# Attention and two expert layers on one core: the first batch's P·v product in plain float32

## The chip, the core and the metric

The kernel runs on one NeuronCore of a Trainium2 chip. TensorE (PE, with its weight loads listed as PEld) multiplies, VectorE (DVE) and ScalarE (ACT) work elementwise, GpSimd (POOL) works elementwise and issues indirect DMAs, and SyncE (SP) issues the other DMAs. The metric is the device time of one execution in microseconds (us).

## The reference

The inputs are q, k and v of 4 batches with 8 heads each, 576 positions and 64 features, and the weights of two feed-forward stages. All of it is float32.

```python
scores = scale * np.matmul(q, k.transpose(0, 1, 3, 2))
scores = np.where(mask, scores, -1000000000.0)      # mask: block_i >= block_j, blocks of 64
scores = scores - np.max(scores, axis=-1, keepdims=True)
attn = np.exp(scores)
attn = attn / (np.sum(attn, axis=-1, keepdims=True) + 1e-09)
out = np.matmul(attn, v)
...
x = out.transpose(0, 2, 1, 3).reshape(B * S, H * D)
x = ((x @ w1) * (x @ w2)) @ w3 @ w_out
...
# then a router (noisy top 2 of 8 experts) and, per expert, relu(x @ w1[e]) @ w2[e], weighted
```

## The kernel before

**Split products.** Most products are made from float32r operands. A float32 matrix is split into a high part (a rounded copy, by ACT) and a low part (the difference, by DVE or POOL), and two or three matmuls of the parts are summed in PSUM (`split`, `mm3`). For P·v two parts of P meet one weight tile that holds v's high part in columns 0 to 63 and its low part in columns 64 to 127, so the output has 128 rows; they go to DRAM (`x2`) and a later stage adds the two halves.

**One head of attention.** `load` and `load_v` bring q, k and v. `prep_h` splits q and k (ACT, DVE L571, POOL L574), `prep_v` splits v (ACT L579, POOL L580). `s_unit` makes the scores of 128 rows of q at a time in PSUM (`sb`, L599 to L602); `s_max` takes the row maxima (DVE L613, and L616 to join two halves) and the exponentials (ACT L618). `g_unit` transposes P in 128x128 tiles into a PSUM bank (`tp`, L629) in four groups and copies each into `pt`: the high part by ACT (L633), the low part by DVE (L639), or, for group 3 of the first eight heads, by a second ACT copy (L636) and POOL (L637). `av_a` and `av_b` multiply (L645, L656): per head six matmul shapes of 128, 448, 448, 320, 192 and 128 columns, each twice, once per part of P. Head numbers 0 to 7 are the first batch.

**Beside the heads.** While the first ten heads run, four times per head (`feed`) a 512 KB piece of the first feed-forward stage's weights is loaded into one of two buffers `stg` (L511), turned from 64-bit to 32-bit words by three DVE instructions (`conv64`, L520 to L522, into `stf`), and split by ACT (L453) and POOL (L457) into `pc`. The product w3·w_out is made from these pieces in 64 units of three 512-column matmuls (`w_unit`). After it the feed-forward stage itself (`Moe1`) fills PE's time between the heads' steps, in chunks of 256 tokens; its inputs `xab`, `xr` come from `x2` and from the sums of the heads of a whole batch.

**The order.** The tables `FIRST` and `LATER` say in what order steps of head i and head i+1 are recorded; a list scheduler then orders each engine's instructions by its own estimates and the priorities given. Each engine runs its list strictly in that order, so an instruction that waits holds up what stands behind it. `buf` places an odd head of the first batch in pool `px`, all others in `p1`.

Of the kernel before, what the change touches and what calls it, by code (L numbers as in the profile page):

```python
# [8 lines left out]
F32 = mybir.dt.float32  # L9
F32R = mybir.dt.float32r  # L10
# [4 lines left out]
OP = mybir.AluOpType  # L15
# [4 lines left out]
B, H, S, D = 4, 8, 576, 64  # L20
NT, DM, DF, E = 2304, 512, 1024, 8
BH = B * H
P = 128
# [23 lines left out]
PTW = 1792  # L47
AV0 = 1280
# [27 lines left out]
def r32(ap):  # L76
    return ap.bitcast(F32)
# [365 lines left out]
class Kernel:  # L443
# [82 lines left out]
    def attention(self):  # L526
        tc, nc, a = self.tc, self.nc, self.a
        moe1 = self.moe1
        with tc.tile_pool(name="p1", bufs=1, side="right") as p1, tc.tile_pool(name="stg", bufs=2, side="right") as self.stg, \
# [13 lines left out]
            px = pxs.enter_context(tc.tile_pool(name="px", bufs=1))  # L543

            def buf(h, shape, dt, name):

                return (px if h < H and h % 2 else p1).tile(shape, dt, name=name)

            pbs = []
            for h in range(2):  # L550
                pbs.append([buf(h, [P, PW[t]], F32, f"pb{t}") for t in range(5)])
                for t in range(5):
                    if PW[t] > KW[t]:
                        nc.gpsimd.memset(pbs[h][t][:, KW[t]:], 0.0)

            def load(h):
                c = hd[h] = Ctx()
                c.qk = buf(h, [P, 2, S], F32, "qk")
                nc.sync.dma_start(c.qk, a["qk"][h])

            def load_v(h):
                c = hd[h]
                c.v = buf(h, [P, 5, D], F32, "v")
                nc.sync.dma_start(c.v, a["v"][h])

            def prep_h(h):
# [8 lines left out]

            def prep_v(h):
                c = hd[h]
                c.vv = buf(h, [P, 5, P], F32R, "vv")
                nc.scalar.copy(c.vv[:, :, 0:64], c.v)  # L579
                nc.gpsimd.tensor_tensor(c.vv[:, :, 64:128], c.v, r32(c.vv[:, :, 0:64]), op=OP.subtract)  # L580

# [39 lines left out]
            def g_unit(h, g):  # L621
                c = hd[h]
                pb = pbs[h < H and h % 2]
                if g == 0:
                    c.pt = buf(h, [P, 2, PTW], F32R, "pt")
                base, skip, items = G_UNITS[g]
                bank = psT.tile([P, 512], F32, name="tp")
                for n, (t, kt) in enumerate(items):
                    nc.tensor.transpose(bank[:, n * P:(n + 1) * P], pb[t][:, kt * P:(kt + 1) * P], self.ident)  # L629
                o = len(items) * P - skip  # L630
                src = bank[:, skip:skip + o]
                h_, l_ = c.pt[:, 0, base:base + o], c.pt[:, 1, base:base + o]
                nc.scalar.copy(h_, src)  # L633
                if h < H and g == 3:
                    gf = px.tile([P, 512], F32, name="gf", bufs=2)[:, 0:o]
                    nc.scalar.copy(gf, src)  # L636
                    nc.gpsimd.tensor_tensor(l_, gf, r32(h_), op=OP.subtract)  # L637
                else:
                    nc.vector.tensor_tensor(l_, src, r32(h_), op=OP.subtract)  # L639

            def av_a(h):
                c = hd[h]
                bank = psT.tile([P, 512], F32, name="tp")
                for i in range(2):
                    nc.tensor.matmul(bank[:, 0:P], c.vv[:, 0, :], c.pt[:, i, AV0:AV0 + P], start=(i == 0), stop=(i == 1))  # L645
                c.ev = buf(h, [P, S], F32, "ev")
                nc.vector.tensor_copy(c.ev[:, 0:128], bank[:, 0:128])  # L647

            def av_b(h, kts):
                c = hd[h]  # L650
                if kts[0] == 0:
                    c.av = psV.tile([P, 512], F32, name="av")
                for kt in kts:
                    _, s0, w, o0 = AV_UNITS[kt]
                    for i in range(2):
                        nc.tensor.matmul(c.av[:, o0:o0 + w], c.vv[:, kt, :], c.pt[:, i, s0:s0 + w],  # L656
                                         start=(kt == 0 and i == 0), stop=(kt == 4 and i == 1))
                if kts[-1] == 4:
                    nc.scalar.copy(c.ev[:, 128:576], c.av[:, 0:448])
                    self.x2w[h] = nc.sync.dma_start(self.x2[h], c.ev)  # L660
# [93 lines left out]

            tick = moe1.tick
            load(0)
            raw += [self.load64(*jobs[n][:2]) for n in range(2)]
            feed()
            prep_h(0)
            load(1)  # L760
            load_v(0)
            feed()
            feed()

            def step(i, j, op):

                kind, n = op[0], op[1:]
                if kind == "f":
                    fill(float(n))
                elif kind == "c":  # L770
                    feed()
                elif kind == "t":
                    tick()
                elif kind == "g" and i >= 0:
                    g_unit(i, int(n))
                elif kind == "p" and i >= 0:
                    prep_v(i)
                elif kind == "a" and i >= 0:
                    av_a(i)
                elif kind == "b" and i >= 0:  # L780
                    av_b(i, [0, 1, 2] if n == "0" else [3, 4])
                elif kind == "s" and j < BH:
                    s_unit(j, int(n))
                    s_max(j)
                elif kind == "h" and j + 1 < BH:
                    prep_h(j + 1)
                elif kind == "v" and 0 < j < BH:
                    load_v(j)
                elif kind == "l" and j + 2 < BH:
                    load(j + 2)  # L790
                elif kind == "o":
                    if i == H - 1 or i > H and i % H == 0:
                        sums_out((i - 1) // H if i > H else 0)
                    if i >= H:
                        moe1.ready = i // H
                    if i == 4:
                        moe1.setup_dram(0)
# [225 lines left out]
```

## Time and profile before

| what | value |
|---|---|
| median of 3 runs | 1152.62 us (1151.78 to 1153.02) |
| the profiled execution's own time | 1154.8 us |
| its span, first to last instruction | 1152.9 us |
| PE busy | 1059.8 us (92%), 6588 matmuls |
| DVE busy | 588.2 us (51%) |
| ACT busy | 503.5 us (44%) |
| POOL busy | 384.8 us (33%) |
| mean granted TensorE clock | 0.966 |

Busy shares are averages over the whole span; a stage has its own. PE's busy time counts matmuls that overlap each other in the pipeline, so it overstates how full PE is. The granted clock is a share of 2.4 GHz; the two levels seen are 1.0 and 0.5.

### The profile page before, as it was taken

The numbers are of one execution on the slowest core, as the hardware profiler recorded it, in microseconds if no ns is written. First come the engines' busy times: TensorE is split into PE (matmuls) and PEld (weight loads), VectorE is DVE, ScalarE is ACT, GpSimd is POOL, SyncE is SP. The second block draws the span as 40 slices with busy tenths as digits, with TensorE's granted clock in tenths as the row PEclk, the third lists the DMA queues.
The fourth block names the chain that finished last, engine by engine and source line by source line (L and its number), as shares of the span: only waits on it lengthen the run. The fifth ranks groups of instructions, "written<-read, shape, count | busy, mean of one in ns | idle before, by whom it ended". The sixth has DMA issues, their size and how long they took to land.

```text
span 1152.9 us, 17651 instructions
## 1 busy us (share of the span) xinstructions
PE 1059.8 (92%) x6588; PEld 951.2 (83%) x6588; DVE 588.2 (51%) x1253; ACT 503.5 (44%) x1196; POOL 384.8 (33%) x369
## 2 busy tenths in 40 slices
PE   4698978998999987999899988999999999999996
PEld 3486767897898967998888887998989898989894
DVE  5989997765485735645433642542424242424120
ACT  4765565564465635553223432533333333333220
POOL 4654555424242423422322325413131313120202
PEclk8899979999899988999999999999999999999999
DMA  8654586324622355313522317736263626351303
GB/s 243 199 167 165 158 225 196 96 82 91 191 92 83 95 153 138 88 54 91 92 56 37 129 47 230 211 105 150 78 154 89 158 81 150 83 131 28 45 5 44
DMA packets 75347, 135.82 MB, mean 118 GB/s; under 512 B 15885, under 2 KB 41717, under 8 KB 75253
## 3 DMA queue, kind: packets, MB, share of 16 engines
q1 hardware_dynamic: 65141, 113.44, 34.0%
q0 software_dynamic: 10112, 21.16, 9.8%
q8 instruction: 54, 0.88, 0.3%
q14 instruction: 40, 0.33, 0.1%
HBM read 103.92 MB, written 30.66 MB: 117 GB/s over the span
## 4 chain that ended last, share of the span: by engine, by line
PE 66%; DVE 12%; DMA 12%; issue 3%; ACT 2%; POOL 1%; SPq 0%; POOLq 0%; DVEq 0%; ACTq 0%
PE ph L462 12%; PE ph L463 12%; PE ph L464 12%; PE m L462 6%; PE m L463 6%; PE m L464 6%; DMA xr<-rs 3%; PE tp L629 2%; PE av L656 2%; DVE stf L521 2%; DMA stg<-in_w_dram 2%; PE sb L602 2%; DVE hi L571 1%; PE m L871 1%; DVE stf L522 1%
## 5 line engine op out<-in xcount | busy, mean ns | idle before, releaser
L462 PE MATMUL m<-xh,pc 128*128 128x256 f32 x576 | 165.9, 292 | 4.0 <-DVE at L204 3.6
L463 PE MATMUL m<-xh,pc 128*128 128x256 f32 x576 | 163.2, 287 | 0.0
L464 PE MATMUL m<-xh,pc 128*128 128x256 f32 x576 | 163.0, 287 | 0.0
L462 PE MATMUL ph<-xt,pc 128*128 128x256 f32 (+1 forms) x512 | 157.1, 309 | 4.9 <-ACT xt L453 4.9
L463 PE MATMUL ph<-xt,pc 128*128 128x256 f32 (+1 forms) x512 | 157.4, 307 | 0.0
L464 PE MATMUL ph<-xt,pc 128*128 128x256 f32 (+1 forms) x512 | 157.1, 307 | 0.0
L898 POOL DMA_INDIRECT out_dram<-yo,ids x40 | 64.1, 1603 | 202.7 <-ACT yo L897 104.2
L884 DVE SCALAR_TENSOR_TENSOR ht<-ph,ht 128x256 fp32r<-128x256 f32 (+1 forms) x128 | 61.8, 490 | 132.7 <-ACT ht L883 132.7
L462 PE MATMUL ph<-pc,ht 128*128 128x512 f32 x320 | 128.0, 401 | 0.0
L463 PE MATMUL ph<-pc,ht 128*128 128x512 f32 x320 | 126.3, 395 | 0.0
L464 PE MATMUL ph<-pc,ht 128*128 128x512 f32 x320 | 126.1, 395 | 0.0
L453 ACT CAST pc<-stf 128x1024 fp32r<-128x1024 f32 (+1 forms) x96 | 82.0, 871 | 89.4 <-DMA stf<-in_m_dram 47.5
L457 DVE TENSOR_TENSOR pc<-stf,pc 128x1024 fp32r<-128x1024 f32 x56 | 67.3, 1224 | 101.4 <-ACT pc L453 95.1
L618 ACT ACTIVATE pb<-sb,nm 128x320 f32<-128x320 f32 (+3 forms) x192 | 93.6, 496 | 51.4 <-DVE nm L616 25.0
L462 PEld LDWEIGHTS m<-xh,pc 128*128 128x128 f32 x576 | 110.8, 194 | 6.1 <-DVE at L204 5.1
L883 ACT ACTIVATE ht<-ph 128x256 fp32r<-128x256 f32 (+1 forms) x128 | 55.4, 437 | 131.9 <-PE ph L464 131.8
L463 PEld LDWEIGHTS m<-xh,pc 128*128 128x128 f32 x576 | 110.8, 194 | 0.6
L464 PEld LDWEIGHTS m<-xh,pc 128*128 128x128 f32 x576 | 110.4, 193 | 0.4
L457 POOL TENSOR_TENSOR gt<-at,gt 128x256 fp32r<-128x256 f32 x72 | 57.6, 803 | 133.5 <-ACT gt L453 130.8
L462 PEld LDWEIGHTS ph<-xt,pc 128*128 128x128 f32 x512 | 96.6, 189 | 5.5 <-ACT xt L453 5.2
L629 PE MATMUL tp<-ident,pb 128*128 128x128 f32 x480 | 82.5, 289 | 18.6 <-DVE ev L647 8.2
L613 DVE TENSOR_REDUCE nm<-sb 128x1 f32<-128x128 f32 (+2 forms) x192 | 79.7, 437 | 34.3 <-PE sb L602 32.7
(153 smaller groups left out, 2370.6 us busy)
## 6 DMA issues: line engine op xcount, KB each, us to landing
stf<-in_m_dram SPq DMA_DIRECT2D x56, 512.0 KB
qk<-in_qk_dram SPq DMA_DIRECT2D x32, 576.0 KB
stg<-in_w_dram SPq DMA_DIRECT2D x32, 512.0 KB
x<-ev SPq DMA_DIRECT2D x32, 288.0 KB
v<-in_v_dram SPq DMA_DIRECT2D x32, 160.0 KB
xab<-x SPq DMA_DIRECT2D x20, 256.0 KB
yt<-y SPq DMA_DIRECT2D x18, 260.0 KB
stg<-in_w_out_dram SPq DMA_DIRECT2D x8, 512.0 KB
```

The source lines that it names most:

```text
L453: nc.scalar.copy(h, src)
L457: eng.tensor_tensor(l, src, r32(h), op=OP.subtract)
L462: nc.tensor.matmul(out, a, c, start=first, stop=False)
L463: nc.tensor.matmul(out, a, d, start=False, stop=False)
L464: nc.tensor.matmul(out, b, c, start=False, stop=last)
L521: v.scalar_tensor_tensor(fi, wi[:, :, 1], -0x40000000, fi, op0=OP.bitwise_and, op1=OP.bitwise_or)
L613: nc.vector.tensor_reduce(nm[:, n:n + 1], o[:, 0:w], axis=AX, op=OP.max, negate=True)
L618: nc.scalar.activation(pb[t][:, k0:k0 + src.free_size()], src, AF.Exp, bias=nm, scale=1.0, accum_out=sums[:, h // H, t + n, h % H:h % H + 1])
L629: nc.tensor.transpose(bank[:, n * P:(n + 1) * P], pb[t][:, kt * P:(kt + 1) * P], self.ident)
L883: nc.scalar.activation(hh[:, 0, f, :], ph, AF.Relu)
L884: nc.vector.scalar_tensor_tensor(hh[:, 1, f, :], ph, 0.0, r32(hh[:, 0, f, :]), op0=OP.max, op1=OP.subtract)
L898: nc.gpsimd.indirect_dma_start(out=self.a["out"], out_offset=self.idx(e, i), in_=yo, in_offset=None, compute_op=OP.add)
```

## The change

For heads 0 to 7, P·v is one float32 matmul per shape instead of two float32r ones. `pt` keeps one float32 copy of the transposed P (ACT L633 alone), so the low parts by DVE (L639), the extra ACT copy (L636) and POOL's part (L637) are gone for these heads. v is loaded straight into columns 0 to 63 of one of two weight tiles `vz`, whose other columns POOL sets to zero once at the start, so `prep_v` has nothing to do for these heads and the DMA writes 256-byte pieces instead of 1280-byte ones. `pt` of these heads now comes from `px` with two buffers. Heads 8 to 31 keep the two parts.

```diff
+            vz = []
+            for h in range(2):
+                vz.append(px.tile([P, 5, P], F32, name=f"vz{h}"))
+                nc.gpsimd.memset(vz[h], 0.0)
+
...
             def load_v(h):
                 c = hd[h]
-                c.v = buf(h, [P, 5, D], F32, "v")
+                if h < H:
+                    c.vv = vz[h % 2]
+                    nc.sync.dma_start(c.vv[:, :, 0:D], a["v"][h])
+                    return
+                c.v = p1.tile([P, 5, D], F32, name="v")
                 nc.sync.dma_start(c.v, a["v"][h])
...
             def prep_v(h):
                 c = hd[h]
-                c.vv = buf(h, [P, 5, P], F32R, "vv")
+                if h < H:
+                    return
+                c.vv = p1.tile([P, 5, P], F32R, name="vv")
...
                 if g == 0:
-                    c.pt = buf(h, [P, 2, PTW], F32R, "pt")
+                    if h < H:
+                        c.pt = px.tile([P, 1, PTW], F32, name="pt", bufs=2)
+                    else:
+                        c.pt = p1.tile([P, 2, PTW], F32R, name="pt")
...
                 nc.scalar.copy(h_, src)
-                if h < H and g == 3:
-                    gf = px.tile([P, 512], F32, name="gf", bufs=2)[:, 0:o]
-                    nc.scalar.copy(gf, src)
-                    nc.gpsimd.tensor_tensor(l_, gf, r32(h_), op=OP.subtract)
-                else:
-                    nc.vector.tensor_tensor(l_, src, r32(h_), op=OP.subtract)
+                if h >= H:
+                    nc.vector.tensor_tensor(c.pt[:, 1, base:base + o], src, r32(h_), op=OP.subtract)
...
-                    for i in range(2):
+                    m = c.pt.shape[1]
+                    for i in range(m):
                         nc.tensor.matmul(c.av[:, o0:o0 + w], c.vv[:, kt, :], c.pt[:, i, s0:s0 + w],
-                                         start=(kt == 0 and i == 0), stop=(kt == 4 and i == 1))
+                                         start=(kt == 0 and i == 0), stop=(kt == 4 and i == m - 1))
```

The scheduler makes new lists from this for the time in which the heads run; behind the last head the lists are the same.

On DVE, in the middle of the first batch before (the `pt` rows are the low parts of P, `nm` the maxima of the scores, `stf` the weight words):

```order
L613 TENSOR_REDUCE nm_723<-sb 128x1
L639 TENSOR_TENSOR pt<-tp,pt 128x448
L613 TENSOR_REDUCE nm_730<-sb 128x1
L520 TENSOR_SCALAR stf<-stg 128x512
L613 TENSOR_REDUCE nm_773<-sb 128x1
L521 SCALAR_TENSOR_TENSOR stf<-stg,stf 128x512
L639 TENSOR_TENSOR pt<-tp,pt 128x448
L613 TENSOR_REDUCE nm_773<-sb 128x1
L522 SCALAR_TENSOR_TENSOR stf<-stg,stf 128x512
```

On DVE, the same head's stretch now (the maxima stand on L626, the conversion of the words on the lines it had):

```order
L626 TENSOR_REDUCE nm_669<-sb 128x1
L520 TENSOR_SCALAR stf<-stg 128x512
L521 SCALAR_TENSOR_TENSOR stf<-stg,stf 128x512
L626 TENSOR_REDUCE nm_676<-sb 128x1
L626 TENSOR_REDUCE nm_715<-sb 128x1
L522 SCALAR_TENSOR_TENSOR stf<-stg,stf 128x512
L626 TENSOR_REDUCE nm_715<-sb 128x1
```

The low parts are gone and the rest keeps its order.

On PE, at P·v of a head of the first batch before (`av` is P·v, `tp` a transpose, `m` a unit of w3·w_out, `sb` the next head's scores):

```order
L629 MATMUL tp<-ident,pb_110 128x128
L629 MATMUL tp<-ident,pb_113 128x128
L629 MATMUL tp<-ident,pb_114 128x128 x2
L656 MATMUL av<-pt,vv 128x448 x3
L463 MATMUL m<-pc_70,pc_72 128x512
L464 MATMUL m<-pc_70,pc_72 128x512
L462 MATMUL m<-pc_67,pc_71 128x512
L463 MATMUL m<-pc_67,pc_71 128x512
L599 MATMUL sb<-hi 128x320
```

On PE, at such a place now (P·v stands on L670, the transposes on L645, the scores on L612 to L615):

```order
L645 MATMUL tp<-ident,pb_122 128x128
L645 MATMUL tp<-ident,pb_123 128x128 x2
L670 MATMUL av<-pt,vz_130 128x448 x2
L612 MATMUL sb<-hi 128x288
L614 LDWEIGHTS mkl
L614 MATMUL sb<-mkr,mkl 128x64
L615 MATMUL sb<-kl,hi 128x288
L612 MATMUL sb<-hi 128x192
```

The two long products now stand once each and directly ahead of the next scores; units of w3·w_out stand further back. When head 7's last product has its turn, 64 units of `m` stood ahead of it before, and 48 now; one head later it is 64 and 63.

## Rows read from the trace of the kernel before

**Rows 1.** Busy time by stretch (us, records): PE, PEld, DVE, ACT, POOL; clock, DMA

```profile
25.00:145.00 120.00, 99.89 (x534) 80.80 (x532) 113.49 (x185) 74.60 (x196) 65.25 (x48) 0.93 0.55 179
145.00:206.00 61.00, 50.26 (x324) 45.06 (x325) 53.16 (x94) 37.62 (x101) 34.54 (x26) 0.86 0.75 205
206.00:262.00 56.00, 54.54 (x395) 50.07 (x394) 36.80 (x88) 34.86 (x103) 17.27 (x16) 1.00 0.28 86
262.00:320.00 58.00, 51.48 (x336) 46.45 (x335) 29.71 (x68) 27.67 (x79) 20.01 (x18) 0.91 0.56 137
```

**Rows 2.** The chain that ended last, 25 to 145 us, share by line

```profile
by line: DVE stf L521 14.1%; DVE stf L520 11.1%; DMA stg<-in_w_dram 9.9%; DVE stf L522 7.5%; issue 7.1%; DVE nm L613 6.8%; DVE pt L639 6.2%; DVE hi L571 4.5%; DMA x<-ev 3.7%; DVE nm L616 2.7%; DVE pc L457 2.1%; PE tp L629 2.0%; PE sb L602 1
```

**Rows 3.** DVE's groups, 25 to 145 us: count, busy us, mean ns, idle before

```profile
L521 DVE SCALAR_TENSOR_TENSOR stf<-stg,stf 128x512 int32<-128x512 int32 x27 | 25.1, 930 | 0.4
L522 DVE SCALAR_TENSOR_TENSOR stf<-stg,stf 128x512 int32<-128x512 int32 x26 | 23.5, 903 | 0.3
L520 DVE TENSOR_SCALAR stf<-stg 128x512 int32<-128x512 int32 x26 | 17.8, 686 | 2.6 <-DMA stg<-in_w_dram 1.8 <-POOL pc L457 0.9
L639 DVE TENSOR_TENSOR pt<-tp,pt 128x448 fp32r<-128x448 f32 x16 | 9.7, 613 | 0.1
L571 DVE SCALAR_TENSOR_TENSOR hi<-qk,hi 64x576 fp32r<-64x576 f32 x7 | 7.5, 1070 | 0.2
L616 DVE TENSOR_TENSOR nm<-nm 128x1 f32<-128x1 f32 x8 | 6.6, 826 | 0.1
L639 DVE TENSOR_TENSOR pt<-tp,pt 128x512 fp32r<-128x512 f32 x8 | 5.4, 680 | 0.0
```

**Rows 4.** Four DVE lines over the whole span: shortest/median/longest ns

```profile
L521 DVE SCALAR_TENSOR_TENSOR stf<-stg,stf x40: 675/694/1671, 9.4 to 207.8; 128x512 int32<-128x512 int32 x40
L520 DVE TENSOR_SCALAR stf<-stg x40: 409/422/1537, 7.9 to 205.4; 128x512 int32<-128x512 int32 x40
L571 DVE SCALAR_TENSOR_TENSOR hi<-qk,hi x32: 755/756/2034, 7.1 to 504.3; 64x576 fp32r<-64x576 f32 x32
L616 DVE TENSOR_TENSOR nm<-nm x32: 142/360/1308, 16.7 to 517.6; 128x1 f32<-128x1 f32 x32
```

**Rows 5.** Instructions in order of time near 130 us: start, length (us)

```profile
130.24 1.30 POOL L457 TENSOR_TENSOR pc<-stf,pc 128x512 fp32r<-128x512 f32 x1 [1.27 <-ACT pc L453]
130.32 1.22 DVE L616 TENSOR_TENSOR nm<-nm 128x1 f32<-128x1 f32 x1
```

**Rows 6.** Two of POOL's groups, 25 to 145 us

```profile
L637 POOL TENSOR_TENSOR pt<-gf,pt 128x384 fp32r<-128x384 f32 x8 | 10.3, 1292 | 7.3 <-ACT gf L636 7.2
L580 POOL TENSOR_TENSOR vv<-v,vv 128x320 fp32r<-128x320 f32 x7 | 7.9, 1122 | 11.0 <-ACT vv L579 7.0 <-PE sb L602 4.0
```

**Rows 7.** Chain pieces of PE matmuls back to back: start, length (us)

```profile
57.15 0.85 PE tp L629 x4
...
212.74 0.60 PE av L656 x3
...
246.74 0.47 PE m L236 x4
...
249.43 0.68 PE tp L629 x6
250.25 0.54 PE m L244 x4
```

**Rows 8.** Busy time, 55 to 60 us, columns as in rows 1

```profile
55.00:60.00 5.00, 3.86 (x16) 3.46 (x17) 4.08 (x9) 3.10 (x11) 1.71 (x2) 0.50 0.69 243
```

**Rows 9.** The router's product L244, all its matmul records

```profile
L244 PE MATMUL m<-fold,lt x36: 257/258/279, 250.2 to 674.7; 32*128 32x16 f32 x36
```

**Rows 10.** What DVE waited for, 25 to 145 us: total, times, longest

```profile
DVE nm L613 <- PE sb L602: 2.7, 5, 0.8
DVE stf L520 <- DMA stg<-in_w_dram: 1.8, 3, 1.0
```

**Rows 11.** Chain piece of a weight load: start, length (us)

```profile
69.75 4.72 DMA stg<-in_w_dram
```

More of the change, by code (lines that the diff above doesn't have):

```diff
@@ L631, in g_unit @@
                 src = bank[:, skip:skip + o]
-                h_, l_ = c.pt[:, 0, base:base + o], c.pt[:, 1, base:base + o]
+                h_ = c.pt[:, 0, base:base + o]
                 nc.scalar.copy(h_, src)
-                if h < H and g == 3:
-                    gf = px.tile([P, 512], F32, name="gf", bufs=2)[:, 0:o]
-                    nc.scalar.copy(gf, src)
-                    nc.gpsimd.tensor_tensor(l_, gf, r32(h_), op=OP.subtract)
-                else:
-                    nc.vector.tensor_tensor(l_, src, r32(h_), op=OP.subtract)
+                if h >= H:
+                    nc.vector.tensor_tensor(c.pt[:, 1, base:base + o], src, r32(h_), op=OP.subtract)
             def av_a(h):
@@ L643, in av_a @@
                 bank = psT.tile([P, 512], F32, name="tp")
-                for i in range(2):
-                    nc.tensor.matmul(bank[:, 0:P], c.vv[:, 0, :], c.pt[:, i, AV0:AV0 + P], start=(i == 0), stop=(i == 1))
+                m = c.pt.shape[1]
+                for i in range(m):
+                    nc.tensor.matmul(bank[:, 0:P], c.vv[:, 0, :], c.pt[:, i, AV0:AV0 + P], start=(i == 0), stop=(i == m - 1))
                 c.ev = buf(h, [P, S], F32, "ev")
@@ L654, in av_b @@
                     _, s0, w, o0 = AV_UNITS[kt]
-                    for i in range(2):
+                    m = c.pt.shape[1]
+                    for i in range(m):
                         nc.tensor.matmul(c.av[:, o0:o0 + w], c.vv[:, kt, :], c.pt[:, i, s0:s0 + w],
-                                         start=(kt == 0 and i == 0), stop=(kt == 4 and i == 1))
+                                         start=(kt == 0 and i == 0), stop=(kt == 4 and i == m - 1))
                 if kts[-1] == 4:
```

## Prediction

> **What bounds the kernel now.** I read the table of busy time by stretch first, because the 51% of DVE and 92% of PE on the page are averages over stages that differ. From 25 to 145 us, when the eight heads of the first batch run, DVE is busy 113.5 of 120 us, PE 99.9, ACT 74.6, POOL 65.3 [rows 1]. From 206 us on PE is the full engine, 54.5 of 56 us, and DVE has room [rows 1]. So the early stage is DVE's, the late one PE's. The chain of the same stretch agrees: its largest pieces are DVE's conversion of weight words (L520 to L522, 32.7% together), with the low parts of P (`pt` L639) at 6.2% [rows 2]. DVE's own waits are small: 2.7 us for scores and 1.8 us for weight loads in 120 us [rows 10]. The chain's 9.9% of weight loads is therefore mostly time in which DVE did other queued work.
>
> The third thing to see is why DVE is so full. L616 handles one element per partition and takes 0.14 us at its shortest, but 0.83 us on average in this stretch [rows 3, 4]; at 130.3 us it lasted 1.22 us and ended with a POOL instruction that had begun just ahead of it and ran 1.30 us [rows 5]. DVE instructions that read SBUF are held up by POOL's.
>
> **The change part by part.**
> *DVE, removed.* 16 low parts of 448 columns at 0.613 us and 8 of 512 columns at 0.680 us [rows 3] stand in the stretch: 9.7 + 5.4 = 15.1 us. Nothing on DVE replaces them, and DVE has next to no idle time that could swallow them.
>
> *POOL, removed.* Eight low parts of P (10.3 us) and seven of v (7.9 us) [rows 6]: 18.2 of POOL's 65.3 us [rows 1]. What this gives DVE is worked out from the stretch of its instructions over their median (for L616 over its shortest): L521 (930 - 694) x 27 = 6.4 us, L522 against the same 694 ns (903 - 694) x 26 = 5.4, L520 (686 - 422) x 26 = 6.9, L571 (1070 - 756) x 7 = 2.2, L616 (826 - 142) x 8 = 5.5 [rows 3, 4]; 26.4 us in all. If it falls with POOL's time, 18.2/65.3 of it goes: 7.4 us. Bounds: 0, if the remaining POOL instructions meet DVE as often as all did, and 18.2, if each removed one had held DVE for its whole length. I take 7.4, since it is the average over all of POOL's work there.
> The Trainium skill (SBUF — State Buffer, section SBUF: two separate sides) says that DVE and GpSimd share a port pair under an exclusive lock that the loser waits out in full. The pair of rows at 130 us agrees. By it the upper bound, 18.2 us, could be reached, and the sum would be 11 us better; that is a rival below.
>
> *ACT, removed.* A copy of v and a second copy per head. ACT is busy 74.6 of 120 us, and I count nothing for it.
>
> *PE, changed.* Twelve float32r matmuls per head become six float32 ones. The trace has no long float32 product, so I price it from back-to-back pieces at the full clock. Float32r: 448 columns take 0.60/3 = 0.20 us, and a 256-column one 0.47/4 = 0.117, which I use as the floor of a short one [rows 7]. Per head before: 2 x (0.20 + 0.20 + 0.143 for 320 columns + 3 x 0.117) = 1.79 us. Float32: the router's small product is 18 matmuls in the program (two per chunk, nine chunks) and 36 records in the trace [rows 9], so a float32 matmul runs as two; each takes at least 0.54/4 = 0.135 us [rows 7]. A float32 transpose of 128 columns takes 0.68/6 = 0.113 us [rows 7], 0.88 ns per column, twice float32r's 0.45. Two records at 0.88 ns per column: 0.79 us for 448 columns, 0.57 for 320, 0.34 for 192, 0.27 for 128. Per head now: 2 x 0.79 + 0.57 + 0.34 + 2 x 0.27 = 3.03 us, so 1.24 more, 9.9 us for eight heads, 10.7 at the stretch's clock of 0.93 [rows 1]. Bounds: at the lower level a transpose takes 0.85/4 = 0.21 us at a clock of 0.50 [rows 7, 8], everything doubles, and eight heads pay about 20 us more; if a float32 record cost what a float32r one does and there were one, they would save 8 x 1.79/2 = 7.2 us.
> A rule that speaks against the change: the Trainium skill (FP8 and Floating Point Precision, section TensorE Precision Notes) counts four passes through the array for true FP32. Two records at twice the time per column are those four passes, so rows and rule give the same sum here.
> How much of the 10.7 us shows? PE stood idle 20.1 of 120 us in this stretch and 10.7 of the next 61 [rows 1], and its list now puts 16 units of w3·w_out, 48 matmuls, behind the last head of the batch, out of the way of the heads. But the stretch is to shrink, and P·v now stands directly ahead of the scores that DVE's maxima wait for; that wait is 2.7 us today [rows 10]. I charge 4 us, between 0 and 10.7.
>
> *Loads.* Freed DVE time brings the next weight load nearer: one took 4.72 us from issue to landing [rows 11], with two buffers. One piece costs DVE 422 + 694 + 694 = 1.81 us undisturbed [rows 4], so a buffer can turn every 6.5 us and a piece every 3.3 us; now one passes every 120/26.5 = 4.5 us, and after 22 us less every 3.7. That holds on average, not everywhere, so the present 1.8 us of waiting [rows 10] grows; I charge 2.5 us. v comes in 256-byte pieces, five times as many. v is 160 KB per head against 2048 KB of weights, so even at five times the price it adds a third to a DMA share of 0.55 [rows 1]: hidden. The first v load must wait for POOL's two zero fills; behind it on SP stand constants needed much later. Two POOL fills of 640 columns are not in the trace; by 1.29 us per 384 columns [rows 6] they are 4.3 us at most, at least 0, while POOL has nothing to do yet; I count 0. A later v load waits for the products two heads back, long done.
>
> *Sum.* 15.1 + 7.4 = 22.5 us off DVE, less 4 for PE and 2.5 for loads: 16 us. The stage after 206 us is PE's and starts that much earlier with the same work left, so the lead reaches the end. The profiled execution took 1154.8 us (span 1152.9): it would take 1138.8. It lies 2.2 us above the median of 1152.62, so the median should be 1136.6; I say 1137.
>
> **The rivals.**
> *PE sets the batch's pace.* For it: PE's 20.1 idle us shrink by the gain and must still take 10.7. Against it: busy PE records overlap, so PE is emptier than 99.9 us says, and the list has moved units away. Then most of the 10.7 comes off: 22.5 - 10.7 - 2.5 = 9, down to 4 if DVE's waits for scores grow with it: about 1145, up to 1148.5.
> *The weight loads set the pace.* Two buffers and the 4.72 us load: if DVE's freed time turns into waiting for landings, the gain is under 2 us, about 1152. Against it: the average above.
> *Slower: the four-fold product at the lower clock.* If PE falls to the lower level through the batch, as it did at 55 to 60 us, the products cost 20 us more; PE then paces the heads as soon as that exceeds its idle 20.1 us less what DVE gives, so DVE's gain is not realised and some 5 us are lost: 1158. Against it: the stretch's clock is 0.93, and from 206 us it is 1.00 [rows 1].
> *More than forecast.* Either float32 costs less than two records (PE gives 7 us back), or POOL's removed work frees DVE up to its whole length, as the port lock would allow: 15.1 + 18.2 - 6.5 = 27 us, 1126. Against it: 26.4 us of delay against 65.3 us of POOL says that most POOL time holds nobody.
>
> **How the numbers follow.** Forecast (gain 10 to 22 us) 0.60; PE's pace 0.20; load pace 0.06; slower 0.06; more 0.08. The forecast's own range is 1130.5 to 1142.5. The range over cases: low 1128, where part of "more" is left out; high 1148, the end of PE's pace. Repeated runs lie within 0.1% of each other, so 0.2% (2.3 us) is what can be told from no change. Faster: 0.60 + 0.20 + 0.08, and a third of the load case, 0.90. Same: two thirds of it, 0.04. Slower: 0.06.
>
> **What would show it.** Between 25 us and the end of head 7's products DVE's busy time should be lower by 20 us or more, with mean L520 to L522 and L616 shorter; the last conversion, now near 206 us, should come near 190. P·v of 448 columns should appear as two records at about 0.4 us spacing. The time from the last head to the end should be unchanged. The forecast is wrong if the last conversion comes early and the end does not, if L521 stays at 0.93 us, or if DVE's waits for `sb` or `stg` rise by more than 10 us.

## The result, and the profile after

The changed kernel took 1136.06 us in median (1133.57 to 1139.48, 4 runs), the kernel before 1152.2 (1150.68 to 1153.02): a ratio of 0.986, 95% interval 0.9834 to 0.9885. A second timing gave 0.9808 (0.9784 to 0.9832). The two intervals do not meet; the kernel before differs more between the two lots of runs (1152.2 and 1155.3 us) than the changed one (1136.06 and 1134.3), and why is not known. The prediction was 1137 us, range 1128 to 1148. The time came out; the way there did not, as the rows show. The kernel before took 1152.2 to 1156.6 us in median from one lot of runs to the next, so runs are compared below by their ratio to it within a lot; 0.1% is 1.15 us.

Busy time by stretch of the changed kernel, columns as in [rows 1] (length, PE, PEld, DVE, ACT, POOL, clock, DMA share, GB/s):

```profile
25.00:145.00 120.00, 107.94 (x556) 84.14 (x555) 100.54 (x166) 71.03 (x188) 52.75 (x37) 0.94 0.65 195
145.00:206.00 61.00, 50.26 (x303) 44.74 (x304) 53.77 (x92) 34.86 (x94) 34.11 (x25) 0.80 0.67 194
206.00:262.00 56.00, 56.00 (x410) 51.99 (x410) 35.18 (x90) 35.09 (x103) 16.47 (x16) 1.00 0.29 89
262.00:320.00 58.00, 52.03 (x351) 47.51 (x350) 32.56 (x74) 30.91 (x90) 21.83 (x19) 0.91 0.52 134
```

In the first batch DVE is busy 13.0 us less and POOL 12.5 less, and PE's idle time fell from 20.1 to 12.1 us [rows 1]. DVE now has 19.5 idle us: it is no longer the full engine. But from 145 to 206 us the table is nearly the old one, with PE's granted clock at 0.80 after 0.86; what the lower clock costs there no run isolates.

DVE's groups of the same stretch, which answer to [rows 3] (count, busy us, mean ns; idle before):

```profile
L522 DVE SCALAR_TENSOR_TENSOR stf<-stg,stf 128x512 int32<-128x512 int32 x25 | 21.1, 846 | 0.4
L521 DVE SCALAR_TENSOR_TENSOR stf<-stg,stf 128x512 int32<-128x512 int32 x25 | 20.5, 822 | 0.4
L520 DVE TENSOR_SCALAR stf<-stg 128x512 int32<-128x512 int32 x26 | 16.1, 619 | 6.9 <-DMA stg<-in_w_dram 3.7 <-POOL pc L457 2.1 <-DMA stg<-in_w_out_dram 0.9
L582 DVE SCALAR_TENSOR_TENSOR hi<-qk,hi 64x576 fp32r<-64x576 f32 x7 | 8.4, 1201 | 0.2
...
L629 DVE TENSOR_TENSOR nm<-nm 128x1 f32<-128x1 f32 x8 | 5.4, 670 | 0.1
```

The conversions got shorter as POOL got lighter, but they wait 6.9 us instead of 2.6, for landings and for POOL to release `stf`, and one fewer of them is done in the stretch. What DVE waits for there, as in [rows 10]:

```profile
DVE nm L626 <- PE sb L615: 4.8, 6, 1.6
DVE xr L186 <- POOL xab L183: 3.9, 1, 3.9
DVE stf L520 <- DMA stg<-in_w_dram: 3.7, 5, 1.9
DVE stf L520 <- POOL pc L457: 2.1, 3, 1.6
```

The 3.9 us are new: with head 7 done earlier, DVE's list comes to the input `xr` of the feed-forward stage's chunk 0 before POOL has its `xab` ready.

The float32 product: its records, and two places in order of time (start, length in us):

```profile
L670 PE MATMUL av<-pt,vz x80: 272/434/955, 21.1 to 123.5; 128*128 128x448 f32 x32, 128*128 128x320 f32 x16, 128*128 128x192 f32 x16, 128*128 128x128 f32 x16
```

```profile
54.66 0.92 PE L670 MATMUL av<-pt,vz 128*128 128x448 f32 x2
...
55.74 0.92 PE L670 MATMUL av<-pt,vz 128*128 128x448 f32 x2
```

32 records of 448 columns for 16 matmuls: two each. A pair takes 0.92 us from first start to last end, of which the second record adds 0.38 (the first alone shows 0.54).

Now the surprise. A few marks tell how far a run has come. For the kernel before: the copies of the last product of head 7 (the first batch's last) and of head 31, and the feed-forward stage's first two outputs, which are chunk 0, and its last one (L220), all on ACT in order of time:

```profile
146.82 0.53 ACT L659 COPY ev<-av 128x448 f32<-128x448 f32 x1
...
225.59 0.59 ACT L220 COPY y<-m 128x512 f32<-128x512 f32 x1 [0.97 <-PE m L464]
...
232.34 0.63 ACT L220 COPY y<-m 128x512 f32<-128x512 f32 x1
...
529.97 0.53 ACT L659 COPY ev<-av 128x448 f32<-128x448 f32 x1 [0.65 <-PE av L656]
...
664.66 1.07 ACT L220 COPY y<-m 128x512 f32<-128x512 f32 x2 [6.43 <-PE m L464]
```

For the changed kernel:

```profile
124.46 0.53 ACT L673 COPY ev<-av 128x448 f32<-128x448 f32 x1
...
225.18 0.63 ACT L220 COPY y<-m 128x512 f32<-128x512 f32 x1
...
227.25 0.58 ACT L220 COPY y<-m 128x512 f32<-128x512 f32 x1 [1.44 <-PE m L464]
...
502.48 0.53 ACT L673 COPY ev<-av 128x448 f32<-128x448 f32 x1 [2.02 <-PE av L670]
...
644.28 1.07 ACT L220 COPY y<-m 128x512 f32<-128x512 f32 x2 [6.69 <-PE m L464]
```

Head 7 ends 22.4 us earlier, about the 22.5 us that I had worked out for DVE. Then most of the lead goes: the first output is 0.4 us early and the second, which ends chunk 0, 5.1 us. And it grows again, to 20.4 us at the last output. A lead of some 5 us at 230 us cannot be all of what reaches the end.

PE's idle time says the same. From 206 us to the last output, before and now:

```profile
206.00:664.66 458.66, 430.80 (x3019) 395.36 (x3017) 247.83 (x684) 218.64 (x603) 149.34 (x147) 0.97 0.37 97
```

```profile
206.00:644.28 438.28, 423.95 (x2999) 389.38 (x2998) 248.27 (x679) 214.51 (x594) 148.90 (x145) 0.98 0.39 100
```

27.9 idle us have become 14.3. So 13.6 of the 20.4 us are idle time behind 206 us; the other 6.8 are what is left of 11.8 us of idle time ahead of it (8.0 of them from 25 to 145 us) when the 5.0 us by which PE is busy longer in all are taken off.

Where the late part comes from is a wait. PE in 370 to 460 and 520 to 600 us before:

```profile
370.00:460.00 90.00, 77.43 (x547) 71.20 (x546) 50.70 (x134) 46.16 (x136) 28.38 (x26) 0.92 0.45 127
520.00:600.00 80.00, 73.87 (x507) 67.67 (x505) 34.22 (x109) 22.01 (x53) 25.79 (x26) 0.98 0.39 86
```

And now:

```profile
370.00:460.00 90.00, 85.86 (x627) 78.83 (x626) 63.14 (x166) 51.40 (x152) 31.23 (x30) 0.98 0.53 138
520.00:600.00 80.00, 77.62 (x540) 71.22 (x539) 29.54 (x103) 20.86 (x51) 30.73 (x31) 1.00 0.32 63
```

PE idled 12.6 and 6.1 us there, and 4.1 and 2.4 now: 12.2 us. What PE and DVE waited for in 370 to 460 us before (total us, times, longest):

```profile
PE tp L645 <- DVE pt L639: 7.3, 1, 7.3
PE tp L629 <- DVE ev L647: 4.1, 1, 4.1
```

```profile
DVE xr L186 <- DMA xr<-rs: 8.4, 1, 8.4
DVE xr L186 <- POOL xab L183: 7.0, 1, 7.0
```

Chunk 4 of the feed-forward stage is the first that needs tokens of batch 2 (heads 16 to 23). DVE's list reached its input `xr` before those heads' sums had been written out and read back, stood there for 8.4 us, and what PE needed from DVE for the next head stood behind it: 4.1 us of PE's wait. The other 7.3 us stood behind chunk 5's input, for which DVE waited on POOL's `xab`. Chunk 4's input on DVE, before and now:

```profile
420.18 1.23 DVE L186 TENSOR_TENSOR xr<-xab,xr 128x1024 f32<-128x1024 f32 x1 [8.44 <-DMA xr<-rs]
```

```profile
398.86 1.22 DVE L186 TENSOR_TENSOR xr<-xab,xr 128x1024 f32<-128x1024 f32 x1
```

Now DVE does not wait for it. It still waits 8.3 us for chunk 5's, but PE waits for no `ev` or `pt` in that time. The scheduler, given other prices in the first batch, wrote another list for the rest: ahead of head 23's last product stood 294 groups of three matmuls (L462) of the feed-forward stage before, and 273 now; ahead of head 31's, 459 and 428. The heads of batch 2 come earlier relative to that stage, and the wait shrinks. Contrary to the text ahead of the prediction, the lists behind the last head are therefore not the same: 31 more of these groups stand there, and from head 31's copy to the end of the span it is 629.3 us now and was 622.9.

So two theories went to the chip: **R**, the relief of DVE and POOL in the first batch reaches the end; **L**, the list for the later heads makes most of the gain, and in the first 206 us something other than DVE sets the pace.

### The profile page after: what moved, and what is told of

Read it like the earlier page. It is cut to its first block, busy times and chain, and to the rows that moved or that the text cites. A ratio compares the mean times of both kernels' runs of the same rounds, so it can differ in the third digit from the quotient of the medians.

```text
span 1131.8 us, 17580 instructions
## 1 busy us (share of the span) xinstructions
PE 1064.8 (94%) x6588; PEld 950.7 (84%) x6588; DVE 576.9 (51%) x1229; ACT 495.2 (44%) x1180; POOL 371.4 (33%) x355
## 4 chain that ended last, share of the span: by engine, by line
PE 72%; DMA 11%; DVE 10%; issue 3%; ACT 2%; POOL 2%; SPq 1%; POOLq 0%; DVEq 0%; ACTq 0%
PE ph L462 12%; PE ph L464 12%; PE ph L463 12%; PE m L462 7%; PE m L464 7%; PE m L463 7%; PE tp L645 3%; PE av L670 3%; DMA xr<-rs 2%; PE sb L615 2%; PE sb L612 2%; DMA stg<-in_w_dram 2%; PE m L885 2%; DVE stf L521 1%; DVE hi L582 1%
## 5 line engine op out<-in xcount | busy, mean ns | idle before, releaser
L462 PE MATMUL m<-xh,pc 128*128 128x256 f32 x576 | 166.4, 293 | 4.4 <-DVE at L204 2.0
L462 PE MATMUL ph<-xt,pc 128*128 128x256 f32 (+1 forms) x512 | 157.0, 308 | 4.6 <-ACT xt L453 4.6
L462 PE MATMUL ph<-pc,ht 128*128 128x512 f32 x320 | 128.0, 401 | 0.0
L631 ACT ACTIVATE pb<-sb,nm 128x288 f32<-128x288 f32 (+3 forms) x192 | 93.6, 497 | 73.8 <-DVE nm L629 38.8
L462 PEld LDWEIGHTS m<-xh,pc 128*128 128x128 f32 x576 | 110.6, 193 | 6.9 <-DVE at L204 2.9
L457 POOL TENSOR_TENSOR gt<-at,gt 128x256 fp32r<-128x256 f32 x72 | 60.4, 841 | 140.2 <-ACT gt L453 137.7
L462 PEld LDWEIGHTS ph<-xt,pc 128*128 128x128 f32 x512 | 96.6, 189 | 5.2 <-ACT xt L453 4.9
L463 PEld LDWEIGHTS ph<-xt,pc 128*128 128x128 f32 x512 | 96.6, 189 | 0.3
L464 PEld LDWEIGHTS ph<-xt,pc 128*128 128x128 f32 x512 | 96.6, 189 | 0.0
```

The costliest lines, as they stand in the source:

```text
L457: eng.tensor_tensor(l, src, r32(h), op=OP.subtract)
L462: nc.tensor.matmul(out, a, c, start=first, stop=False)
L463: nc.tensor.matmul(out, a, d, start=False, stop=False)
L464: nc.tensor.matmul(out, b, c, start=False, stop=last)
L631: nc.scalar.activation(pb[t][:, k0:k0 + src.free_size()], src, AF.Exp, bias=nm, scale=1.0, accum_out=sums[:, h // H, t + n, h % H:h % H + 1])
```

## The experiments

| run | what it is | list at head 23 | ratio, 95% interval | first and last output, us |
|---|---|---|---|---|
| before | | 294 | 1 | 225.6, 664.7 |
| change | | 273 | 0.986 (0.9834 to 0.9885); again 0.9808 (0.9784 to 0.9832) | 225.2, 644.3 |
| e1 | change, 24 one-column DVE ops | 294 | 0.9965 (0.9945 to 0.9986) | 221.2, 658.0 |
| e2 | before, later fill 2.5 | 264 | 0.9936 (0.9914 to 0.9958) | 227.7, 659.3 |
| e3 | one float32r product | 294 | 0.9905 (0.9871 to 0.9939) | 217.0, 657.0 |
| e4 | change, DVE work back | 294 | 0.9977 (0.9954 to 0.9999) | 223.4, 658.5 |
| e6 | change, POOL work back | 271 | 0.9851 (0.9821 to 0.988) | 233, 655 |
| e7 | e3, DVE work back | 294 | 0.9994 (0.9972 to 1.0016) | 227.0, 668.9 |
| e8 | change, later fill 2.5 | 254 | 0.9807 (0.9783 to 0.9831) | 228, 647 |
| e9 | third `stf` buffer, 7 `gt` | 280 | 0.9895 (0.9867 to 0.9923) | 216.2, 653.3 |
| e10 | third `stg` buffer, 6 `gt` | 280 | 0.9929 (0.9902 to 0.9956) | 214, 659 |
| e11 | change, 7 `gt` | 264 | 0.9881 (0.9863 to 0.9899) | 230, 658 |
| e12 | third `stf` buffer, 2 `y` | 277 | 0.9856 (0.9836 to 0.9877) | 216, 643 |

The outputs are from one profiled execution each.

**e1: the change's work, the old late list.**

```diff
                 if h >= H:
                     nc.vector.tensor_tensor(c.pt[:, 1, base:base + o], src, r32(h_), op=OP.subtract)
+                elif g < 3:
+                    lo = px.tile([P, 512], F32R, name="lo", bufs=2)
+                    nc.vector.tensor_tensor(lo[:, 0:1], src[:, 0:1], h_[:, 0:1], op=OP.subtract)
```

> The change, with one added DVE subtraction of a single column per transposed group 0 to 2 of the first eight heads (24 in all, into a scratch tile). The work is the change's within 3 us of DVE time, but the scheduler's list from head 15 on becomes that of the kernel before: 294 groups of the feed-forward stage's three matmuls stand ahead of head 23's last product, where the change has 273. Theory R (the relief of DVE and POOL in the first batch is carried to the end): 1136 to 1139 us, 13 to 16 below before. Theory L (most of the gain comes from the list that puts heads of batch 2 ahead of the feed-forward stage, so that its chunk 4 waits less for them at 380 to 450 us): 1143 to 1148, and PE idle again 10 us or more between 370 and 450 us.

0.9965: 4 us of gain, less than either theory said. Its stretches 370 to 460 and 520 to 600 us:

```profile
370.00:460.00 90.00, 77.34 (x548) 71.38 (x548) 54.04 (x153) 46.73 (x138) 28.88 (x27) 0.92 0.45 130
520.00:600.00 80.00, 74.16 (x510) 67.84 (x508) 37.17 (x134) 20.97 (x53) 25.71 (x25) 0.98 0.36 81
```

PE's 12.7 and 5.8 idle us are back to those of before. e1's list within the first batch is not quite the change's (56 units of w3·w_out stand ahead of head 7's last product, 48 there), but chunk 0 ends level with the change's (227.25 us) and the last output comes 13.7 us later:

```profile
227.67 0.63 ACT L220 COPY y<-m 128x512 f32<-128x512 f32 x1
...
658.03 1.07 ACT L220 COPY y<-m 128x512 f32<-128x512 f32 x2 [6.21 <-PE m L464]
```

From 206 us to its last output PE idles 27.6 us, against 27.9 in the kernel before. The same relief in the first batch, with the old late list, loses 12 to 18 us of the change's gain. R falls.

**e2: before, with heads ahead.**

```diff
-LATER = "g0 g1 f2.6 o g2 p t c g3 t t t s0 s1 s2 t c t a f2.6 s3 b0 t t c f2.6 c t b1 h v l"
+LATER = "g0 g1 f2.5 o g2 p t c g3 t t t s0 s1 s2 t c t a f2.5 s3 b0 t t c f2.5 c t b1 h v l"
```

> The kernel before, with the fill budget of the later heads at 2.5 instead of 2.6. Up to head 11 its PE list is that of before; at head 23 it has 264 groups of the feed-forward stage ahead instead of 294, so the heads are ahead as in the change, without any relief in the first batch. Theory R: within 3 us of before, 1150 to 1155. Theory L: 1141 to 1147, with PE idle under 6 us between 380 and 450 us instead of 12.6.

0.9936, 7 us, with no change to the first batch at all.

```profile
370.00:460.00 90.00, 85.72 (x609) 77.84 (x608) 55.61 (x143) 53.10 (x155) 30.44 (x28) 0.96 0.49 132
520.00:600.00 80.00, 78.86 (x561) 72.48 (x560) 34.33 (x117) 21.35 (x54) 29.74 (x29) 1.00 0.34 71
```

PE's idle time in the two stretches shrinks to 4.3 and 1.1 us, 13.3 us less than before. Part is given back: from 262 to 320 us PE idles 11.0 us here and 6.5 before. L holds for the direction, though the time stays just outside its range; the list alone does not give the change's whole late gain.

**e3, e4 and e7: what DVE and PE are worth in the first batch.** e4 puts e1's subtraction over all columns (`lo[:, 0:o], src, h_`). e3 takes the float32 price away:

```diff
-                vz.append(px.tile([P, 5, P], F32, name=f"vz{h}"))
+                vz.append(px.tile([P, 5, P], F32R, name=f"vz{h}"))
...
+                    nc.scalar.copy(c.vv[:, :, 0:D], c.v)
...
-                        c.pt = px.tile([P, 1, PTW], F32, name="pt", bufs=2)
+                        c.pt = px.tile([P, 1, PTW], F32R, name="pt", bufs=2)
```

e7 is e3 with e4's DVE work.

> The first batch's P and v are rounded to float32r by ACT and multiplied by one float32r matmul per shape; their low parts are left out. DVE and POOL are relieved as in the change, PE does half of before's product instead of double. Its late list is that of before (294 at head 23). Theory R with 4 us charged to PE: 1131 to 1134. Theory L: 1140 to 1146, since the late wait is back. If PE's float32 price is what ate the first batch's lead, the stage from 206 us on starts at least 8 us earlier than in the change.

> The change, with DVE's 24 subtractions of the low parts of P (16 of 448 and 8 of 512 columns) done again for the first eight heads into a scratch tile that nothing reads. Late list as before (294 at head 23). Theory R: 15 us of DVE time come back, 1148 to 1153. Theory L: also 1148 to 1153, but against the run with 24 single columns (same late list) the difference is DVE's price alone: 10 to 15 us by R, under 6 by L.

> The single float32r product of the first batch (low parts left out), with DVE's 24 subtractions done again into a scratch tile. Late list as before (294). Without the float32 price PE has room. If PE's price is what hid DVE's 15 us in the pair with the float32 product (1151.5 with and 1151.3 without), the 15 us must cost something here: 5 us or more over the 1144.5 of the run without them. If less than 3 us, DVE did not pace the first 206 us, even with PE relieved.

All four (with e1) have the old late list, so they compare the first batch. DVE's work in e4, by the same view as above:

```profile
L654 DVE TENSOR_TENSOR lo<-tp,pt 128x448 fp32r<-128x448 f32 x14 | 8.6, 617 | 0.6 <-ACT pt L649 0.6
L654 DVE TENSOR_TENSOR lo<-tp,pt 128x512 fp32r<-128x512 f32 x8 | 5.5, 683 | 0.0
```

These 14 us cost 0.0012 where PE has the float32 product (e4 against e1, 1.4 us, no difference that these runs can tell), and 0.0089, 10 us, where it has not (e7 against e3). PE's float32 price costs 0.0060, 7 us, with DVE relieved (e1 against e3), and nothing with DVE loaded (e4 against e7). Neither engine paces the batch alone: whichever is lightened, the other is there. By the intervals of e1 and e3 the 7 us could be 2 to 11. e3's first output came 8.2 us before the change's, as its expectation had it, but its chunk 0 ended only 3.7 us before (223.54 us).

**e6: POOL's work back.**

```diff
+                elif g == 3:
+                    lo = px.tile([P, 512], F32R, name="lo", bufs=2)
+                    nc.gpsimd.tensor_tensor(lo[:, 0:o], h_, h_, op=OP.subtract)
...
                 if h < H:
+                    lv = px.tile([P, 5, D], F32R, name="lv")
+                    nc.gpsimd.tensor_tensor(lv, c.vv[:, :, 0:D], c.vv[:, :, 0:D], op=OP.subtract)
                     return
```

> The change, with POOL's removed work done again for the first eight heads into scratch tiles nobody reads: 8 subtractions of 384 columns and 8 of 320. Its list is close to the change's (271 groups ahead of head 23 against 273). Theory R (first-batch relief reaches the end): DVE's conversion instructions go back from a mean of 0.82 to about 0.93 us and 7 us are lost, 1143 to 1146. Theory L (the first batch is paced by PE and the late list gives most of the gain): the means go back as well, but the end moves by less than 4 us, 1136 to 1140.

The change was timed again in the same lot:

> The changed kernel itself, timed again beside its variants. Both theories: the ratio of the first timing, 0.983 to 0.989.

```profile
L521 DVE SCALAR_TENSOR_TENSOR stf<-stg,stf 128x512 int32<-128x512 int32 x24 | 22.6, 940 | 0.5
```

The mean goes from 822 back to 940 ns (930 before), so POOL's work stretches it here. How much it does depends on which instructions meet: in e3, whose POOL is as light as the change's (53.2 us busy from 25 to 145 us against 52.8), the mean is 910. 0.0043 against the change in the same lot, 5 us: between what the two theories said, and the runs cannot tell it from either.

**e8: the list pushed further.** The change with `f2.5`.

> The change, with the later heads' fill budget at 2.5: the list goes further the same way, 254 groups of the feed-forward stage ahead of head 23 (273 in the change, 294 before), 400 ahead of head 31 (428, 459). Theory L, if more of it helps: 1131 to 1135. If the wait at chunk 4 is all there was to gain: within 3 us of the change, since PE idles only 4.1 us between 370 and 460 us there. Theory R: no difference.

0.9807 against 0.9808: nothing more to gain from it.

**e9 to e12: the loop of two buffers.** In e1 DVE waited 8.4 us in the first batch for POOL to release a `stf` buffer:

```profile
DVE stf L520 <- POOL pc L457: 8.4, 6, 3.3
```

e9 gives `stf` a third buffer and e10 gives `stg` one; memory forces a buffer or two less of `gt`. Both lower the later fill budget, to 2.4 and 2.3, and e10 issues its loads three ahead; the cut shows the buffers of e9.

```diff
-        f = self.stg.tile([P, 512], F32, name="stf")
+        f = self.stg.tile([P, 512], F32, name="stf", bufs=3)
...
-        gt = self.gts[c, f] = self.p2b.tile([P, 2, CH], F32R, name="gt", bufs=8)
+        gt = self.gts[c, f] = self.p2b.tile([P, 2, CH], F32R, name="gt", bufs=7)
```

> The change with a third buffer for the converted weight words (stf), paid for by 7 instead of 8 buffers of the feed-forward stage's products (gt), and the later fill budget at 2.4 so that the late list stays near the change's (280 groups ahead of head 23). In the run with single columns DVE waited 8.4 us in the first batch for POOL to release stf. If that loop of two buffers holds up the first 206 us: the first chunk's output moves from 225 us to 218 or earlier, and the end to 1126 to 1131. If PE's float32 price alone paces it: first output within 3 us, end 1133 to 1139.

> The change with a third buffer for loaded weight pieces (stg), loads issued three ahead, 6 instead of 8 buffers gt, later fill budget 2.3 (280 groups ahead of head 23). If the weight loads with two buffers hold up the first 206 us: DVE's waits for landings in 25 to 145 us (3.7 us in the change) fall under 1 us, the first output moves from 225 us to 218 or earlier and the end to 1126 to 1131. If not: within 3 us, end 1133 to 1139.

Last conversions of the changed kernel and of e9 (L522; the last start is behind "to"):

```profile
L522 DVE SCALAR_TENSOR_TENSOR stf<-stg,stf x40: 618/691/1680, 9.6 to 208.0; 128x512 int32<-128x512 int32 x40
```

```profile
L522 DVE SCALAR_TENSOR_TENSOR stf<-stg,stf x40: 671/692/1680, 9.9 to 198.4; 128x512 int32<-128x512 int32 x40
```

A third `stf` buffer brings the last conversion and the first output 9 us forward, and e12 below does it again. DVE's subtractions moved the first output by 2.3 us beside the float32 product (e4 against e1) and by 9.9 without it (e7 against e3). So in the change the weights' loop of two buffers, more than DVE, sets when the feed-forward stage can start. Which wait in the loop it is, the traces do not settle: from 25 to 145 us e9's DVE waits longer for landings (9.4 us against the change's 3.7) and for POOL (3.3 against 2.1), and only from 145 to 206 us less (0.2 us for landings against 5.1). In e10 the waits for landings fell from 3.7 us to nothing and the first output came 11.6 us earlier, as its first case had it. But in both the end came later than the change's. e11 and e12 asked whether the lost `gt` buffers took it:

> The change with 7 instead of 8 buffers gt and nothing else (264 groups ahead of head 23). The run with a third stf buffer had its first output 9 us earlier than the change and ended about 9 us later. If the missing gt buffer took that back: 1140 to 1146. If it was the list behind it: within 3 us of the change, 1133 to 1139.

> The change with a third stf buffer, all 8 buffers gt, 2 instead of 3 buffers y (outputs of the feed-forward stage) to pay for it, and the later fill budget at 2.5 (277 groups ahead of head 23). If the 9 us at the first output reach the end once gt is whole: 1124 to 1130, and a version that beats both. If the later stages take them back whatever the buffers: 1133 to 1143.

Seven `gt` buffers, with the new list that they bring (264), cost 0.2 to 0.7% against the two timings of the change. With `gt` whole and two `y` buffers instead (e12), the first output keeps its 9 us, but at the last output 1 us of lead is left and the ratio is 0.9856, that of the change's first timing. The later stages took it back; what in them did was not isolated. No run beat the change.

## Why the prediction was right in the number and wrong in the way

*What bounds the kernel.* Half right. DVE was the fullest engine of the first batch, but not its only pace: with the float32 product on PE, DVE's subtractions could come back for 1.4 us (e4 against e1), and with DVE lightened, a lighter PE (e3) or a third buffer for the weights (e9) brought the first output forward. I had the loop at a piece every 3.3 us against 3.7 needed and took an average margin of a tenth for cover.

*DVE, 15.1 us.* The work that goes was right; from 25 to 145 us DVE's busy time fell by 13.0 us only, as later work (chunk 0's `xr`, 2.0 us, and `xh`, 2.2) moved into the stretch. Head 7's lead of 22.4 us, for 22.5 worked out with POOL's part, looks like a proof and is luck. 16 units of w3·w_out moved behind that head, by an estimate 11 us of PE's time (48 matmuls of 512 columns, which follow each other every 0.23 us at 404 us of the kernel before). e4, with the same 48 units ahead and DVE's subtractions back, ends head 7 only 2.1 us later than the change:

```profile
126.54 0.53 ACT L676 COPY ev<-av 128x448 f32<-128x448 f32 x1 [3.14 <-PE av L673]
```

So most of that lead is the order and not DVE's subtractions. That the freed time reaches the end was wrong too: 1.4 us of it did (e1 against e4).

*POOL, 7.4 us.* Right in size for this kernel. By the drop of the means in [rows 3], (930 - 822) x 25 + (903 - 846) x 25 + (686 - 619) x 26 + (826 - 670) x 8 = 7.1 us, less 0.9 for L571's line, whose mean rose; 5 us showed at the end when POOL's work came back (e6). But the same sum that gave 26.4 us of delay before gives 24.6 in e3 and 17.9 in e4, both with POOL's work taken away as in the change, so a share of POOL's time is only a rough guide. The Trainium skill's exclusive lock (SBUF — State Buffer, section SBUF: two separate sides) stands with [rows 5] and e6; the upper bound of 18.2 us that I drew from it was not reached.

*PE, 1.24 us per head.* Two records per matmul, the second 0.38 us behind the first for 448 columns, as worked out. I charged 4 us for 9.9 us more of PE time. e3 against e1 prices a larger step, a float32 product against one float32r one: 3.03 less 0.90, so 17 us for eight heads, which cost 7. By that share the charge of 4 was about right, an estimate.

*Loads, 2.5 us.* From 25 to 145 us the waits for landings rose from 1.8 us to 4.6 (3.7 and 0.9), as charged. Mis-sized all the same, since the buffers hold up more than these waits show: the third one moved the first output by 9 us (e9). And the later loads of v were not free, as I had it: on SP's queue they waited 6.4 us for P·v of the heads before, three times, the longest 3.2 us.

*The step that failed:* "The stage after 206 us is PE's and starts that much earlier with the same work left, so the lead reaches the end." Chunk 0 ended 5.1 us earlier, its first output 0.4, where the sum had 16. The relief with its prices was worth 4 us (e1). And the work that was left did not stay in its order. The other 12 to 18 us go with the new list for the later heads, which is the one thing from head 15 on in which e1 and the change differ; I had compared the lists only up to one head behind the first batch. I had PE's idle time of 370 to 460 us in the trace and did not ask what ended it. e2 shows that 7 us of this can be had without the change; whether the rest needs the first batch's work or only a better list is open.

*The marks I named.* DVE's busy time from 25 us to head 7's end fell from 115.8 to 84.8 us, more than the 20 I had asked for, but that stretch is itself 22 us shorter by the order; over the same 120 us it fell by 13.0. The last conversion started at 208.0 us (209.5 before), not near 190. The time from the last head to the end was to be unchanged and grew by 6.4 us. By the last two the theory stood wrong before any experiment, although the time was met. And repeated runs do not lie within 0.1% of each other: the kernel before ran from 1150.2 to 1160.9 us in one lot.

## What to carry to other kernels

Where a scheduler writes the lists, a change to one stage rewrites the stages behind it: compare the lists to the end, by counts of one kind of work ahead of another, and read what ends every idle stretch of the bounding engine. A predicted total that is met proves little; check a mark in the middle, and run the change's work with the old list. Where two engines and a buffer loop lie within a tenth of each other, as here, freeing one of them buys only the distance to the next. And a mark that comes at the forecast time can come there by the order alone: ask whether the same work stands ahead of it.

## What the runs showed of the hardware that was not expected

A float32 matmul of 448 columns runs as two records, the second of which adds 0.38 us at the full clock. An instruction for one element per partition on DVE (the join of the maxima) took 0.83 us on average beside a busy POOL and 0.67 with POOL lightened, but 0.28 to 0.78 in the other runs with a light POOL (e7 and e1 at the ends). DVE's low parts of P, which take one operand from PSUM, kept their length: 613 ns for 448 columns before and 617 in e4, with POOL busy 65.3 and 47.7 us of the 120. Five times as many DMA pieces for v, 256 bytes each, show no price: the DMA share from 25 to 145 us is 0.65 in the change and 0.65 in e3, which loads v in pieces of 1280 bytes. Nothing else was unexpected.
